# Seven products for four in a part of the first MLP layer of the last two token groups

## The chip, the cores and the metric

The kernel runs on one core of a Trainium2 chip. Times are device microseconds (us) of that core from launch to end; the number compared is the median over several runs. The profile is one further execution with the hardware profiler; its span reaches from the first to the last instruction.

## The reference

Causal attention with 16 extra "beacon" keys, then an MLP with a quick gelu. The operands come as float32.

```python
B, H, S, Nb, D = (8, 8, 576, 16, 64)
scores = scale * np.matmul(q, k_all.transpose(0, 1, 3, 2))   # k_all: beacon_k, k
scores = np.where(causal, -1000000000.0, scores)
a = np.exp(scores - scores.max(-1, keepdims=True))
a /= a.sum(-1, keepdims=True) + 1e-09
attn_out = np.matmul(a, v_all)
...
x = attn_out.transpose(0, 2, 1, 3).reshape(B * S, H * D)     # 4608 x 512
h = x @ w_in                                                 # w_in  512 x 2048
g = h * (1.0 / (1.0 + np.exp(-1.702 * h)))
return g @ w_out                                             # w_out 2048 x 512
```

## The kernel before

The kernel is one stream of instructions for each engine, written out by a planner while the program is built. Each piece of work is an `op` with an engine, an estimated duration, the pieces that it depends on, a priority and at times a due time. `Plan.run` (L65) goes through them as a list scheduler would and so fixes the order on each engine; the semaphores between engines follow from the tiles read and written. On the chip nothing is reordered: an engine takes its instructions in that order and waits where an operand is late.

**Attention** goes in 16 sets (8 batches, two halves of the heads). A set's scores are made in chunks by TensorE (`e_qk`, L448) into one tile of four PSUM banks, `s`; ScalarE takes the exponent into an SBUF tile `E` (L466), of which there are three in rotation; GpSimd masks (L490); VectorE sums over keys (L502); TensorE multiplies with V (`e_av`, L539), and VectorE normalizes into `xT` (L574), which holds x transposed, in f16, for four batches of tokens. There are 55 chunks. VectorE also transposes Q and K (L429).

**The MLP** goes in ten groups of tokens: groups 0 and 1 of 256, groups 2 to 9 of 512. The first layer (`e_m1`, L593, with its matmul at L604) makes 16 tiles of 128 rows of h for a group, each from four matmuls of 512 columns, each tile in one of the four other PSUM banks ("the ring", `u`). ScalarE's gelu (L625) writes the tile into `g`. The second layer of groups 2 to 9 is already done by Strassen's scheme in Winograd's form (`products`, L958): VectorE makes sums of quarters of g in `sA` (L669, f16; one set of tiles, so a group's sums begin when the group before has had its products), sums of quarters of w_out in `tB` once, TensorE makes seven products (`e_prod`, L704, L718), each of 16 matmuls of 256 columns, and they are put together by one scaled copy on ScalarE (L729) and seven joins on VectorE (L734), which add a product in PSUM to a part in SBUF. Four DMAs a group then store the result (L741).

**What sets the order around the change.** `QUOTAS` (L271) holds, for groups 2 to 9, the number of chunks after which the group's first layer is opened; while it is open ("inside"), no further chunk is issued and first-layer tiles go ahead of second-layer ones. `choose` (L191) picks TensorE's next piece: chunks first, then attention values that have waited for 7000 ns, then first-layer tiles if inside, otherwise first- and second-layer pieces in turn. `ring_free` (L55) gives the bank of the ring that is free first. `due_of` (L750) spreads the sets between `T_ATT0` and `T_ATT1` (L746): Q and K transposes are due 12 us before a set, loads of Q and K 22 us, of V 12 us. `NEAR` (L14) is how long VectorE is kept for urgent work, `IDLE` (L15) how long TensorE may stand idle before a group is opened early, `TDUE` (L948) when the sums of w_out are due. Groups 8 and 9 are tokens 3584 to 4095 and 4096 to 4607; both need attention of the last batch.

Of the kernel before, what the change touches and what calls it, by code (L numbers as in the profile page):

```python
# [10 lines left out]
ALU = mybir.AluOpType  # L11


NEAR = 500  # L14
IDLE = 800  # L15


class Op:
# [6 lines left out]
class Plan:  # L25
# [4 lines left out]

    def __init__(self, ring):
        self.ops = []
        self.bank = [None] * ring
        self.tiles = {}
        self.closers = {}
        self.quota = {}
# [15 lines left out]
        self.ops.append(o)  # L52
        return o

    def ring_free(self):  # L55
        best = None
        for i, key in enumerate(self.bank):
            t = 0
            for c in self.closers[key] if key is not None else ():
                t = None if t is None or c.start is None else max(t, c.end + 60)  # L60
            if t is not None and (best is None or t < best[0]):
                best = (t, i)
        return best

    def run(self):  # L65
# [8 lines left out]
        group, inside, ntile, nchunk = min(self.quota), False, 0, 0  # L74
        firsts = {}
        for o in self.ops:
            if o.kind == "m1":
                firsts.setdefault(o.pr, o)

        left_of = {}  # L80
        for o in self.ops:
# [3 lines left out]
        def allowed(o):  # L85
            if o.kind == "m2" and o.ring not in self.tiles:
                if sum(left_of[k] > 0 for k in self.tiles if k in left_of) >= 2:
                    return False
            if o.kind == "m1":
                return o.pr < group or (o.pr == group and (inside or group not in self.quota))  # L90
            if o.kind == "qk":
                return not inside
            if o.table is not None and o.table != table:
                return due_of_table[table] == 0
            return True
# [3 lines left out]
        while todo:  # L99
            best = None  # L100
            if not inside and group in self.quota:
                f = firsts[group]
                inside = nchunk >= self.quota[group] and f.left == 0
            slot = self.ring_free()
            ringt = slot[0] if slot else None
            for e, cand in avail.items():
                t = None
                for o in cand:
                    if not allowed(o):
                        continue  # L110
                    r = max(o.ready, o.due)
                    if o.ring is not None and o.ring not in self.tiles:
                        if ringt is None:
                            continue
                        r = max(r, ringt)
                    if t is None or r < t:
                        t = r
                if t is not None:
                    t = max(t, free[e])
                    if best is None or t < best[0]:  # L120
                        best = (t, e)
            assert best is not None, [(o.name, o.eng) for o in self.ops if o.start is None][:40]
            t, e = best
            if e == "PE" and not inside and t > free[e] + IDLE and group in self.quota:
                f = firsts[group]
                if f.left == 0 and f.ready <= t:
                    inside = True
                    continue
            ok = []
            for o in avail[e]:  # L130
                if not allowed(o):
                    continue
                r = max(o.ready, o.due)
                if o.ring is not None and o.ring not in self.tiles:
                    if ringt is None:
                        continue
                    r = max(r, ringt)
                if r <= t:
                    ok.append(o)
            if e == "PE":  # L140
                o = self.choose(ok, t, mode, last, free, inside)
            else:
                o = min(ok, key=lambda o: (o.pr, o.ready, o.seq))
                if e == "DVE" and o.pr > 0:
                    near = [x for x in avail[e] if x.pr == 0 and max(x.ready, x.due) <= t + NEAR]
                    if near:
                        o = min(near, key=lambda o: (o.ready, o.seq))
                        t = max(t, o.ready, o.due)
            dur = o.dur
            if e == "PE":  # L150
                if o.mode != mode:
                    dur += 95 + 0.75 * tail / 2.4
                mode, last, tail = o.mode, o.kind, o.tail
                if o.ring is not None and o.ring not in self.tiles:
                    self.tiles[o.ring] = slot[1]
                    self.bank[slot[1]] = o.ring
            if o.kind == "m1":
                ntile += 1 if o.pr == group else 0
                if inside and ntile == 16:
                    group, inside, ntile = group + 1, False, 0  # L160
# [12 lines left out]
            o.start, o.end = t, t + dur  # L173
            free[e] = o.end
            avail[e].remove(o)
            order.append(o)
            todo -= 1
            for u in o.users:
                u.left -= 1
                lat = self.LAT[o.eng] if u.eng != o.eng or o.eng == "Q" else 0  # L180
                if u.eng == "Q":
                    lat = 300 if o.eng == "SP" else 1200
                elif o.name == "bk" and o.eng != "DVE":
                    lat = 2500
# [6 lines left out]
    def choose(self, ok, t, mode, last, free, inside):  # L191
# [12 lines left out]
                return av  # L204
        if qk:
            return qk
        late = first(("av",), lambda o: o.ready + 7000 <= t)
        if late:
            return late
        m1, m2 = first(("m1",)), first(("m2",))  # L210
# [8 lines left out]
def kernel(  # L219
# [11 lines left out]
    nc = tc.nc  # L231
# [36 lines left out]
    w2t = cst.tile([P, NNT, DMODEL], F16, tag="w2", name="w2")  # L268
    XR = 4 * S
    NPL, NPE, GEL = 2, 10, 2  # L270
    QUOTAS = (19, 28, 38, 42, 48, 55, 55, 55)  # L271
    HM, HN = 256, NNT // 2
    xT = cst.tile([P, NKT, XR], F16, tag="xT", name="xT")
    sA = [cst.tile([P, HN, HM], F16, tag=f"sA{i}", name=f"sA{i}") for i in range(3)]
    tB = [cst.tile([P, HN, HM], F16, tag=f"tB{i}", name=f"tB{i}") for i in range(3)]
# [80 lines left out]
    rings, Es, ss, gts, zs, zsum = {}, {}, {}, {}, {}, {}  # L356

    plan = Plan(RING)

    def ring_tile(key):  # L360
        if key not in rings:
            i = plan.tiles[key]
            rings[key] = psu.tile([P, 512], F32, tag=f"u{i}", name=f"u{i}")
        return rings[key]


# [223 lines left out]
        GROUPS.append((t, min(NTOK, t + 512)))  # L590
    NG = len(GROUPS)

    def e_m1(g, n0, n1):  # L593
        t0, t1 = GROUPS[g]
        w = t1 - t0
        if g not in gts:
            gts[g] = gp.tile([P, NNT, 512], F16, tag="g", name="g")
        u = ring_tile(("m1", g, n0))
        for nt in range(n0, n1):
            o = (nt - n0) * w  # L600
# [75 lines left out]
    def e_t(i, eng):  # L676
# [9 lines left out]
        else:  # L686
            add(eng, t3, b22, b12, ALU.subtract)

    def quarter(g, i, j):
        return gts[g][:, HN * j : HN * (j + 1), HM * i : HM * (i + 1)]  # L690

# [169 lines left out]
    def values(s):  # L861
# [96 lines left out]
    def products(g):  # L958
        eng = "POOL" if g < SDVE else "DVE"
        sd = {}  # L960
        for n0 in range(0, HN, SQ):
            n1 = n0 + SQ
            prev = []
            for i in range(4):
                deps = prev + done.get(g - 1, [])
                for n in range(n0, n1):
                    deps += [gates[(g, n)], gates[(g, n + HN)]]
# [8 lines left out]
        def prod(p):  # L976
            prev = []
            for n0 in range(0, HN, SQ):
                deps = list(prev)
                if lhs[p] is not None:  # L980
                    deps.append(sd[(lhs[p], n0)])
                else:
                    deps += [gates[(g, n + (HN if p in (2, 4) else 0))] for n in range(n0, n0 + SQ)]
                if rhs[p] is not None:
                    deps.append(tds[rhs[p]])
                o = op(
# [34 lines left out]
        store(c12, "m", 0, 1)  # L1021
        ends[g] = c12

    def mlp(g):
        if g == NPL and NPL < NPE:
            weights()
# [108 lines left out]
```

## Time and profile before

| | us |
|---|---|
| median of 3 runs (331.37 to 331.89) | 331.48 |
| the profiled execution | 331.71 |
| its span | 330.0 |
| PE busy | 311.5 (94%) |
| DVE busy | 237.5 (72%) |
| ACT busy | 203.6 (62%) |
| POOL busy | 116.9 (35%) |
| granted TensorE clock | 1.000 |

PE is TensorE's matmuls, PEld its weight loads, DVE VectorE, ACT ScalarE, POOL GpSimd, SP the engine that issues the stores. The end of a matmul is modelled, and matmuls overlap, so PE's busy time alone doesn't say whether it is at its peak; the distance between starts in a long run of equal matmuls does. A row names the line, the operation, what it writes and reads and in which shape, how often, and in brackets how long the engine stood idle before it and what ended that. The order of the stages from 245 us on, as TensorE's timeline has it:

| stage | from (us) | to (us) |
|---|---|---|
| first layer of group 7, with the key sums of set 15 between | 245.8 | 260.1 |
| three products of group 7's second layer | 260.1 | 266.3 |
| attention values of set 15 | 266.3 | 267.8 |
| first layer of group 8 | 267.8 | 281.6 |
| the other products of group 7 | 281.6 | 287.7 |
| first layer of group 9 | 287.7 | 301.5 |
| second layer of group 8 | 301.5 | 313.8 |
| second layer of group 9 | 313.8 | 326.2 |
| last join, store, end | 326.2 | 330.0 |

### The profile page before, as it was taken

The numbers are of one execution on the slowest core, as the hardware profiler recorded it, in microseconds if no ns is written. First come the engines' busy times: TensorE is split into PE (matmuls) and PEld (weight loads), VectorE is DVE, ScalarE is ACT, GpSimd is POOL, SyncE is SP. The second block draws the span as 40 slices with busy tenths as digits, with TensorE's granted clock in tenths as the row PEclk, the third lists the DMA queues.
The fourth block names the chain that finished last, engine by engine and source line by source line (L and its number), as shares of the span: only waits on it lengthen the run. The fifth ranks groups of instructions, "written<-read, shape, count | busy, mean of one in ns | idle before, by whom it ended". The sixth has DMA issues, their size and how long they took to land. (4 is left out here: it accounts for less than half of the span.)

```text
span 330.0 us, 9837 instructions
## 1 busy us (share of the span) xinstructions
PE 311.5 (94%) x4288; PEld 210.9 (64%) x4288; DVE 237.5 (72%) x478; ACT 203.6 (62%) x234; POOL 116.9 (35%) x178
## 2 busy tenths in 40 slices
PE   0699899999999999999999999999999999999995
PEld 0477666545885467646878877447774664746884
DVE  4847959796998788987999589978896630460484
ACT  1676487787767786777758586858677427175000
POOL 8765557572238205360427046702422000000000
PEclk9999999999999999999999999999999999999999
DMA  7999999569017903392149623930120000110122
GB/s 126 161 205 208 200 178 156 83 105 130 29 41 140 145 2 82 89 129 50 47 95 127 85 53 89 127 85 2 34 96 3 2 32 2 46 51 2 66 96 95
DMA packets 58219, 28.81 MB, mean 87 GB/s; under 512 B 41280, under 2 KB 53568, under 8 KB 58176
## 3 DMA queue, kind: packets, MB, share of 16 engines
q0 software_dynamic: 47552, 18.49, 47.7%
q1 hardware_dynamic: 10560, 9.69, 8.9%
q8 instruction: 33, 0.54, 0.7%
q14 instruction: 10, 0.08, 0.1%
q10 hardware_dynamic: 64, 0.01, 0.0%
HBM read 37.22 MB, written 9.44 MB: 141 GB/s over the span
## 5 line engine op out<-in xcount | busy, mean ns | idle before, releaser
L604 PE MATMUL u<-xT,w 128*128 128x512 f16 (+1 forms) x704 | 130.7, 343 | 2.1 <-DVE g L637 1.1
L469 ACT ACTIVATE E<-s 128x2048 f16<-128x2048 f32 (+4 forms) x66 | 98.8, 1514 | 42.7 <-PE s L458 42.0
L604 PEld LDWEIGHTS <-w 128*128 128x128 f16 x704 | 68.0, 98 | 58.5 <-issue 3.2
L625 ACT ACTIVATE g<-u 128x512 f16<-128x512 f32 x128 | 74.4, 598 | 43.2 <-PE u L604 43.0
L490 POOL TENSOR_SCALAR_AFFINE_SELECT E<-E 128x512 f16<-128x512 f16 (+3 forms) x78 | 52.0, 689 | 119.9 <-ACT E L469 116.2
L734 DVE SCALAR_TENSOR_TENSOR osb<-u,osb 128x512 f32<-128x512 f32 x56 | 37.4, 680 | 40.5 <-PE u L718 26.9
L718 PEld LDWEIGHTS <-g 128*128 128x128 f16 x512 | 48.6, 98 | 7.3 <-issue 0.2
L458 PE MATMUL s<-qT,kT 32*128 32x32 f16 (+20 forms) x1376 | 35.9, 235 | 11.7 <-DVE qT L429 10.3
L718 PE MATMUL u<-w,g 128*128 128x256 f16 x384 | 46.0, 273 | 0.0
L458 PEld LDWEIGHTS <-kT 32*128 32x128 f16 x1376 | 26.0, 95 | 29.1 <-issue 14.7
L718 PEld LDWEIGHTS <-sA 128*128 128x128 f16 x384 | 36.4, 98 | 4.9
L718 PE MATMUL u<-tB,sA 128*128 128x256 f16 x256 | 31.3, 273 | 0.0
L389 POOL DMA_DIRECT2D vb<-in_v_dram x32 | 27.3, 866 | 2.5 <-DMA kn<-in_k_dram 1.5
L545 PE MATMUL u<-E,vb 128*32 128x352 f16 (+8 forms) x928 | 27.7, 267 | 0.0
L580 DVE TENSOR_TENSOR xT<-u,rz 128x352 f16<-128x352 f32 (+2 forms) x52 | 24.9, 518 | 1.7 <-PE u L545 1.1
L508 DVE TENSOR_TENSOR zs<-zs,E 128x1344 f16<-128x1344 f16 (+2 forms) x36 | 23.5, 652 | 3.1 <-POOL E L490 0.5
L545 PEld LDWEIGHTS <-vb 128*32 128x32 f16 (+1 forms) x928 | 20.1, 98 | 5.4 <-issue 1.3
L429 DVE STREAM_TRANSPOSE kT<-kn 128x576 f32<-128x576 f32 x16 | 20.1, 1258 | 4.4 <-PE s L458 2.8
L669 DVE TENSOR_TENSOR sA<-g 128x512 f16<-128x512 f16 x32 | 12.8, 417 | 12.2 <-ACT g L625 11.9
L429 DVE STREAM_TRANSPOSE qT<-qn 128x576 f32<-128x576 f32 x16 | 20.0, 1249 | 2.2 <-PE s L458 1.8
L557 DVE STREAM_TRANSPOSE zt<-u 128x352 f32<-128x352 f32 (+2 forms) x32 | 13.8, 459 | 9.0 <-PE u L545 8.9
L718 PE MATMUL u<-tB,g 128*128 128x256 f16 x128 | 16.3, 273 | 0.0
(44 smaller groups left out, 229.1 us busy)
## 6 DMA issues: line engine op xcount, KB each, us to landing
out_dram<-osb SPq DMA_DIRECT2D x36, 256.0 KB, 2.2
kn<-in_k_dram POOLq DMA_DIRECT2D x16, 288.0 KB, 5.6
qn<-in_q_dram POOLq DMA_DIRECT2D x16, 288.0 KB, 6.3
vb<-in_v_dram POOLq DMA_DIRECT2D x24, 128.0 KB, 5.2
w<-in_moe_w_in_dram POOLq DMA_DIRECT2D x8, 256.0 KB, 9.2
w<-in_moe_w_out_dram POOLq DMA_DIRECT2D x4, 512.0 KB, 14.0
vb<-in_v_dram POOLq DMA_DIRECT2D x8, 112.0 KB, 3.7
vb<-in_v_dram POOLq DMA_DIRECT2D x8, 80.0 KB, 5.0
```

Source lines behind the costliest of these rows:

```text
L389: nc.gpsimd.dma_start(out=t[0 : hi - lo, j, h0:h1, :], in_=v[b, h0:h1, lo:hi, :].rearrange("h n d -> n h d"),)
L429: nc.vector.transpose(out=f32(dst.rearrange("p n e -> p (n e)")).rearrange("p (r t) -> p t r", t=TR), in_=f32(src[:, :]).rearrange("p (t c ...
L458: nc.tensor.matmul(sc[:, h, o : o + w], kT[s % NB2][r : r + 32, j * P : (j + 1) * P, d], qT[s % NB2][r : r + 32, a : a + w, d], start=(d = ...
L469: nc.scalar.activation(out=Es[s][:, :, c0:c1], in_=ss[i][:, :, o : o + c1 - c0], func=AFT.Exp, scale=0.125,)
L490: nc.gpsimd.affine_select(out=blk, in_=blk, compare_op=ALU.is_ge, fill=0.0, base=off + (Nb if j == 0 else 0), pattern=[[0, Q], [1, w]], ch ...
L508: nc.vector.tensor_tensor(out=t, in0=E[:, :, Z0:S] if i == 1 else t, in1=E[:, :, wcol[i] : wcol[i] + S - a], op=ALU.add,)
L545: nc.tensor.matmul(u[32 * h : 32 * h + 32, a:e], lhs, src[0:kw, h, col : col + e - a], start=first, stop=last,)
L580: nc.vector.tensor_tensor(out=xT[:, 2 * hs + x : 2 * hs + x + n, t0 : t0 + w], in0=rings[("av", s, x, half)][:, 0 : n * w].rearrange("p (n ...
L604: nc.tensor.matmul(u[:, o + a - t0 : o + e - t0], w1t[:, kp, nt * P : (nt + 1) * P], xT[:, kp, a % XR : (e - 1) % XR + 1], start=(kp == 0) ...
L625: nc.scalar.activation(out=gts[g][:, n0:n1, 0:w], in_=rings[("m1", g, n0)][:, 0 : n * w].rearrange("p (n w) -> p n w", n=n), func=AFT.Gelu ...
L718: nc.tensor.matmul(u[:, HM * mt : HM * (mt + 1)], lhs[:, n, mt * P : (mt + 1) * P], rhs[:, n, :], start=(n == 0 and mt == 0), stop=(n == H ...
L734: nc.vector.scalar_tensor_tensor(out=osbs[(g, dst)][:, :], in0=rings[("p", g, p)][:, :], scalar=scale_of(g), in1=osbs[(g, src)][:, :], op0 ...
```

## The change

In groups 8 and 9 a part of the first layer is made by the same scheme of seven products. h transposed, for one group, is a matrix of 2048 x 512; it is cut into the halves of the 2048 rows (index i), the halves of the 512 tokens (index j) and, along the 512 that are summed over, into two halves. `FIRST` names slices: slice d takes rows 256 d to 256 d + 255 of each half, so four of a group's 16 tiles. Group 8 has slices 0 and 2 done this way, group 9 slices 0, 1 and 2; the other slices stay with `e_m1`. A product (`e_first`) is four matmuls of 256 columns into one bank. The banks are the four of the score tile `s`, taken over once the last exponent has been read out of them (`plan.gate`, `late_s`). Four sums of quarters of w_in (`e_wsum`, once) and four of x (`e_xsum`, once a group) are made in f16 by VectorE, and the parts of a slice (m, a, u) are kept in f32; all of them lie in the three `E` tiles, after the attention values of sets 13, 14 and 15 have been read. Per slice there is one copy on ScalarE, seven joins on VectorE, and four gelus, which read the part in SBUF.

The planner changes too: two lists of free banks; from group 8 on (`MIX`) first-layer tiles of any group are allowed and taken in turn with second-layer pieces (`LATE1` = 0); and its constants are other ones.

```diff
-NEAR = 500
-IDLE = 800
+NEAR = 560
+IDLE = 3000
+MIX = 8
+LATE1 = 0
...
             if o.kind == "m1":
+                if group >= MIX:
+                    return True
                 return o.pr < group or (o.pr == group and (inside or group not in self.quota))
...
-                o = self.choose(ok, t, mode, last, free, inside)
+                o = self.choose(ok, t, mode, last, free, inside and (group < MIX or LATE1))
...
-        late = first(("av",), lambda o: o.ready + 7000 <= t)
+        late = first(("av",), lambda o: o.ready + 5000 <= t)
...
-    QUOTAS = (19, 28, 38, 42, 48, 55, 55, 55)
+    QUOTAS = (20, 27, 33, 33, 47, 54, 55, 55)
+    FIRST = {8: (0, 2, ), 9: (0, 1, 2, )}
...
+            if i < RING:
+                rings[key] = psu.tile([P, 512], F32, tag=f"u{i}", name=f"u{i}")
+            else:
+                if not late_s:
+                    late_s.append(pss.tile([P, Q, 512], F32, tag="s", name="s"))
+                rings[key] = late_s[0][:, i - RING, :]
...
+    def late_tile(i):
+        if i not in lateE:
+            lateE[i] = ep.tile([P, Q, ETOT], F16, tag="E", name="E")
+        return lateE[i][:, :, :].rearrange("p q e -> p (q e)")
...
+        for t in range(2):
+            n = (2 * d + t) * P
+            for k in range(2):
+                nc.tensor.matmul(
+                    u[:, HM * t : HM * (t + 1)],
+                    lhs[:, k, n : n + P],
+                    rhs[:, k, :],
+                    start=(t == 0 and k == 0),
+                    stop=(t == 1 and k == 1),
+                )
+    def e_fcopy(g, d):
+        nc.scalar.copy(out=part(d, "m"), in_=rings[("n", g, d, 1)][:, :])
+    def e_fjoin(g, d, p, src, dst):
+        nc.vector.tensor_tensor(
+            out=part(d, dst), in0=rings[("n", g, d, p)][:, :], in1=part(d, src), op=ALU.add
+        )
...
-    T_ATT0, T_ATT1 = 17000, 249000
+    T_ATT0, T_ATT1 = -1000, 245000
...
-                op("DVE", 75 + 0.517 * 4 * w, deps + sums[-1:], lambda i=i: e_zadd(s, i), pr=3, name="zadd")
+                op("DVE", 75 + 0.6 * 4 * w, deps + sums[-1:], lambda i=i: e_zadd(s, i), pr=3, name="zadd")
...
-    SQ, SDVE, TDUE = 2, 0, 60000
+    SQ, SDVE, TDUE = 2, 0, 70000
...
+        prod(1)
+        m = op(
+            "ACT", 480, [last[1], used.get("m")] + free, lambda: e_fcopy(g, d), pr=1,
+            closes=("n", g, d, 1), name="fcopy",
+        )
+        prod(2)
+        c11 = join(2, "m", "a", [m, used.get("a")] + free)
+        ga = gelu("a", 0, 0, c11)
+        prod(6)
+        u2 = join(6, "m", "m", [c11])
+        prod(7)
+        u3 = join(7, "m", "u", [u2, used.get("u")])
+        prod(4)
+        c21 = join(4, "u", "a", [u3, ga])
+        ga = gelu("a", 1, 0, c21)
+        prod(5)
+        u4 = join(5, "m", "m", [u3], False)
+        c22 = join(5, "u", "u", [c21, u4])
+        gu = gelu("u", 1, 1, c22)
+        prod(3)
+        c12 = join(3, "m", "m", [u4])
+        gm = gelu("m", 0, 1, c12)
...
+            if n0 % HN // SQ in FIRST.get(g, ()):
+                if n0 < HN and n0 % SQ == 0:
+                    first_quarters(g, n0 // SQ, xs, old)
+                continue
...
+    plan.gate = exps[(len(CHUNKS) - 1, len(CHUNKS[-1]) - 1)]
```

More of the change, by code (lines that the diff above doesn't have):

```diff
@@ L32, in __init__ @@
         self.ops = []
-        self.bank = [None] * ring
+        self.bank = [None] * (ring + 4)
+        self.ring = ring
+        self.gate = None
         self.tiles = {}
@@ L53, in op, with ring_free @@
         return o
-    def ring_free(self):
+    def ring_free(self, late):
         best = None
-        for i, key in enumerate(self.bank):
-            t = 0
+        if late and self.gate.start is None:
+            return None
+        for i in range(self.ring, self.ring + 4) if late else range(self.ring):
+            key = self.bank[i]
+            t = self.gate.end + 200 if late else 0
             for c in self.closers[key] if key is not None else ():
@@ L73, in run @@
         table, due_of_table = "e", {"e": 0, "g": 0}
-        group, inside, ntile, nchunk = min(self.quota), False, 0, 0
-        firsts = {}
+        group, inside, nchunk = min(self.quota), False, 0
+        firsts, count = {}, {}
         for o in self.ops:
@@ L78, in run @@
                 firsts.setdefault(o.pr, o)
+                count[o.pr] = count.get(o.pr, 0) + 1
         left_of = {}
@@ L103, in run @@
                 inside = nchunk >= self.quota[group] and f.left == 0
-            slot = self.ring_free()
-            ringt = slot[0] if slot else None
+            slots = [self.ring_free(late) for late in (False, True)]
             for e, cand in avail.items():
@@ L112, in run @@
                     if o.ring is not None and o.ring not in self.tiles:
-                        if ringt is None:
+                        slot = slots[o.ring[0] == "n"]
+                        if slot is None:
                             continue
-                        r = max(r, ringt)
+                        r = max(r, slot[0])
                     if t is None or r < t:
@@ L134, in run @@
                 if o.ring is not None and o.ring not in self.tiles:
-                    if ringt is None:
+                    slot = slots[o.ring[0] == "n"]
+                    if slot is None:
                         continue
-                    r = max(r, ringt)
+                    r = max(r, slot[0])
                 if r <= t:
@@ L154, in run @@
                 if o.ring is not None and o.ring not in self.tiles:
+                    slot = slots[o.ring[0] == "n"]
                     self.tiles[o.ring] = slot[1]
@@ L157, in run @@
             if o.kind == "m1":
-                ntile += 1 if o.pr == group else 0
-                if inside and ntile == 16:
-                    group, inside, ntile = group + 1, False, 0
+                count[o.pr] -= 1
+                if inside and count[group] == 0:
+                    group, inside = group + 1, False
             if o.kind == "m2":
@@ L358 @@
     plan = Plan(RING)
+    late_s = []
     def ring_tile(key):
@@ L362, in ring_tile @@
             i = plan.tiles[key]
-            rings[key] = psu.tile([P, 512], F32, tag=f"u{i}", name=f"u{i}")
+            if i < RING:
[4 more added lines that the diff above has]
+                rings[key] = late_s[0][:, i - RING, :]
         return rings[key]
@@ L591, with group_tile @@
     NG = len(GROUPS)
+    def group_tile(g):
+        if g not in gts:
+            gts[g] = gp.tile([P, NNT, 512], F16, tag="g", name="g")
+        return gts[g]
     def e_m1(g, n0, n1):
@@ L595, in e_m1 @@
         w = t1 - t0
-        if g not in gts:
-            gts[g] = gp.tile([P, NNT, 512], F16, tag="g", name="g")
+        group_tile(g)
         u = ring_tile(("m1", g, n0))
@@ L687, in e_t, with wsum, xsum @@
             add(eng, t3, b22, b12, ALU.subtract)
+    lateE = {}
+    def late_tile(i):
+        if i not in lateE:
+            lateE[i] = ep.tile([P, Q, ETOT], F16, tag="E", name="E")
+        return lateE[i][:, :, :].rearrange("p q e -> p (q e)")
+    def wsum(i):
+        t = late_tile(0)[:, 2048 * i : 2048 * (i + 1)] if i < 3 else late_tile(1)[:, 0:2048]
+        return t.rearrange("p (k n) -> p k n", k=2)
+    def xsum(g, i):
+        o = 2048 * (1 + g % 2) + 512 * i
+        return late_tile(1)[:, o : o + 512].rearrange("p (k w) -> p k w", k=2)
@@ new lines, in part, with wq, xq, e_wsum @@
+    def part(d, x):
+        i = 3 * (d % 2) + "mau".index(x)
+        return f32(late_tile(2)[:, 1024 * i : 1024 * (i + 1)])
+    def wq(i, j):
+        return w1t[:, 2 * j : 2 * j + 2, DFF // 2 * i : DFF // 2 * (i + 1)]
+    def xq(g, i, j):
+        t0 = (GROUPS[g][0] + HM * j) % XR
+        return xT[:, 2 * i : 2 * i + 2, t0 : t0 + HM]
+    def e_wsum(i):
+        s1, s2, s4, s3 = (wsum(x) for x in range(4))
+        if i == 0:
+            add("DVE", s1, wq(1, 0), wq(1, 1), ALU.add)
+        elif i == 1:
+            add("DVE", s2, s1, wq(0, 0), ALU.subtract)
+        elif i == 2:
+            add("DVE", s4, wq(0, 1), s2, ALU.subtract)
+        else:
+            add("DVE", s3, wq(0, 0), wq(1, 0), ALU.subtract)
@@ new lines, in e_xsum, with e_first @@
+    def e_xsum(g, i):
+        t1, t2, t4, t3 = (xsum(g, x) for x in range(4))
+        if i == 0:
+            add("DVE", t1, xq(g, 0, 1), xq(g, 0, 0), ALU.subtract)
+        elif i == 1:
+            add("DVE", t2, xq(g, 1, 1), t1, ALU.subtract)
+        elif i == 2:
+            add("DVE", t4, xq(g, 1, 0), t2, ALU.subtract)
+        else:
+            add("DVE", t3, xq(g, 1, 1), xq(g, 0, 1), ALU.subtract)
+    def e_first(g, d, p):
+        u = ring_tile(("n", g, d, p))
+        lhs, rhs = {
+            1: (wq(0, 0), xq(g, 0, 0)),
+            2: (wq(0, 1), xq(g, 1, 0)),
+            3: (wsum(2), xq(g, 1, 1)),
+            4: (wq(1, 1), xsum(g, 2)),
+            5: (wsum(0), xsum(g, 0)),
+            6: (wsum(1), xsum(g, 1)),
+            7: (wsum(3), xsum(g, 3)),
+        }[p]
+        for t in range(2):
[8 more added lines that the diff above has]
+                )
@@ new lines, in e_fcopy, with e_fgelu @@
+    def e_fcopy(g, d):
[4 more added lines that the diff above has]
+        )
+    def e_fgelu(g, d, x, i, j):
+        n0 = 2 * d + HN * i
+        nc.scalar.activation(
+            out=group_tile(g)[:, n0 : n0 + 2, HM * j : HM * (j + 1)],
+            in_=part(d, x).rearrange("p (t w) -> p t w", t=2),
+            func=AFT.Gelu_apprx_sigmoid,
+        )
@@ L966, in products @@
                 for n in range(n0, n1):
-                    deps += [gates[(g, n)], gates[(g, n + HN)]]
+                    deps += gate(g, n) + gate(g, n + HN)
                 d = 336
@@ L982, in prod @@
                 else:
-                    deps += [gates[(g, n + (HN if p in (2, 4) else 0))] for n in range(n0, n0 + SQ)]
+                    for n in range(n0, n0 + SQ):
+                        deps += gate(g, n + (HN if p in (2, 4) else 0), 1 if p == 4 else 0)
                 if rhs[p] is not None:
@@ L1022, in products, with first_quarters, prod, join @@
         ends[g] = c12
+    wsums = []
+    def first_quarters(g, d, xs, old):
+        every = [(x, h) for x in range(3) for h in range(2)]
+        if not wsums:
+            deps = [avs.get((NSET - 3, x, h)) for x, h in every]
+            for i in range(4):
+                more = [avs.get((NSET - 2, x, h)) for x, h in every] if i == 3 else []
+                wsums.append(op("DVE", 1130, deps + more + wsums[-1:], lambda i=i: e_wsum(i), pr=3, name="wsum"))
+        if (g, 0) not in xsums:
+            deps = xs + [avs.get((NSET - 2, x, h)) for x, h in every]
+            deps += [o for o in m1s.get(g - 2, []) if o.ring[0] == "n"]
+            for i in range(4):
+                xsums[(g, i)] = o = op("DVE", 336, deps, lambda i=i: e_xsum(g, i), pr=2, name="xsum")
+                deps = [o]
+        free = [avs.get((NSET - 1, x, h)) for x, h in every]
+        lhs = {1: None, 2: None, 3: 2, 4: None, 5: 0, 6: 1, 7: 3}
+        rhs = {1: None, 2: None, 3: None, 4: 2, 5: 0, 6: 1, 7: 3}
+        last, used = {}, fused.get(d % 2, {})
+        def prod(p):
+            deps = xs + old + [w for n in (2 * d, 2 * d + 1, 2 * d + HN) for w in w1_of[n]]
+            deps += [wsums[lhs[p]]] if lhs[p] is not None else []
+            deps += [xsums[(g, rhs[p])]] if rhs[p] is not None else []
+            last[p] = op(
+                "PE", 4 * 109, deps, lambda: e_first(g, d, p), kind="m1", pr=g,
+                ring=("n", g, d, p), mode="m", name=f"m1.{g}.{d}.{p}",
+            )
+            m1s.setdefault(g, []).append(last[p])
+        def join(p, src, dst, deps, closes=True):
+            return op(
+                "DVE", 605, [last[p]] + deps, lambda: e_fjoin(g, d, p, src, dst), pr=2,
+                closes=("n", g, d, p) if closes else None, name="fjoin",
+            )
+        def gelu(x, i, j, dep):
+            o = op("ACT", 520, [dep] + old, lambda: e_fgelu(g, d, x, i, j), pr=1, name="fgelu", table="g")
+            for n in (2 * d + HN * i, 2 * d + HN * i + 1):
+                gates.setdefault((g, n), {})[j] = o
+            return o
+        prod(1)
+        m = op(
+            "ACT", 480, [last[1], used.get("m")] + free, lambda: e_fcopy(g, d), pr=1,
+            closes=("n", g, d, 1), name="fcopy",
+        )
+        prod(2)
[15 more added lines that the diff above has]
+        gm = gelu("m", 0, 1, c12)
+        fused[d % 2] = {"m": gm, "a": ga, "u": gu}
@@ L1024, in mlp, with gate @@
+    fused, xsums = {}, {}
+    def gate(g, n, i=None):
+        got = gates[(g, n)]
+        if isinstance(got, dict):
+            return list(got.values()) if i is None else [got[i]]
+        return [got]
     def mlp(g):
```

## The prediction

> **What bounds the kernel now.** I read the windows first, with borders at the ends of the stages that the TensorE timeline shows, and from the last attention product (267.8 us) on. Columns: stretch, its length, then busy us and instructions of PE, PEld, DVE, ACT, POOL, and the clock.
>
> ```profile
> 267.80:281.70 13.90, 13.90 (x73) 6.36 (x66) 0.60 (x2) 8.96 (x15) 0.00 (x0) 1.00 0.00 1
> 281.70:287.80 6.10, 6.10 (x58) 5.46 (x57) 2.67 (x4) 0.60 (x1) 0.00 (x0) 1.00 0.12 43
> 287.80:301.60 13.80, 13.80 (x66) 6.26 (x65) 6.06 (x17) 8.96 (x15) 0.00 (x0) 1.00 0.12 40
> 301.60:313.80 12.20, 12.20 (x114) 10.93 (x113) 4.05 (x6) 1.20 (x2) 0.00 (x0) 1.00 0.13 44
> 313.80:326.20 12.40, 12.37 (x114) 10.84 (x111) 9.93 (x23) 0.60 (x1) 0.00 (x0) 1.00 0.25 85
> 326.20:330.00 3.80, 0.00 (x0) 0.00 (x0) 0.69 (x1) 0.00 (x0) 0.00 (x0) 1.00 0.39 138
> ```
>
> The rows are: first layer of group 8; the rest of group 7's second layer; first layer of group 9; second layers of 8 and of 9; the closing join and store. PE has no gap, while DVE is busy 24.0 of 62.2 us. The chain of waits says the same: from 287.9 on it is matmuls alone, then one join.
>
> ```profile
> 287.90 13.81 PE u L604 x64
> 301.72 24.47 PE u L718 x224
> 326.18 0.02 issue
> 326.21 0.69 DVE osb L734
> ```
>
> It also gives rates: 13.81/64 = 215.8 ns for a 512-column first-layer matmul and 24.47/224 = 109.2 ns for a 256-column Strassen one (a matmul's own row of 379 or 273 ns includes its drain). In this stage a matmul less is time less, as long as every operand is there.
>
> Before it PE is nearly as full. Its waits up to 240 us are one short table; of the matmul's waits only these are over 1 us:
>
> ```profile
> PE s L458 <- DVE qT L429: 10.3, 2, 8.2
> PE s L458 <- ACT E L469: 1.4, 3, 0.6
> PE u L604 <- DVE g L637: 1.1, 1, 1.1
> PE u L604 <- ACT g L625: 1.0, 3, 0.4
> ```
>
> The first is the start (operands arrive), the rest could be reordered away.
>
> **What the Trainium skill says.** "TensorE: Matmul & The Clock Gate", section "Wait — 56ns, not 53.3ns?", gives N/2.4 GHz plus about 2.5 ns: 215.8 and 109.2 ns, exactly the two rates above. "VectorE: DVE Perf Modes", section "The perf-mode tier table", says that a two-tensor operation with a PSUM operand runs at one element a cycle, and with 16-bit SBUF operands at two; the trace has 0.69 us for a 512-column join and 0.42 for a 512-column f16 sum. "PSUM — Partial Sum Buffer", section "PSUM bank collisions raise a hardware error", says two engines may not be in one bank at once, so a product's bank is shut until its last reader is through; no run here shows a collision. "ScalarE: Activation LUTs", section "Table sets: the hidden batching unit", says copy is in every set; the trace agrees: the scaled copy at 303.50 between gelus has no table load beside it.
>
> **The change, part by part.**
>
> *Matmuls.* FIRST takes two of four column pairs of group 8 and three of group 9. One pair is 4 tiles x 4 matmuls of 512 columns, 16 x 215.8 = 3.453 us; as seven products of four 256-column matmuls it is 28 x 109.2 = 3.058. Five pairs save 5 x 0.395 = 1.98 us of PE. Each 256-column matmul has its own weight load (98 ns), which stays beneath 109 as in the second layer.
>
> *Added on DVE.* Seven joins a pair, 35 in all. The nearest row is L734, same shape and types from PSUM and SBUF:
>
> ```profile
> 324.46 1.29 DVE L734 SCALAR_TENSOR_TENSOR osb<-u,osb 128x512 f32<-128x512 f32 x2 [1.05 <-PE u L718]
> 314.59 1.42 DVE L669 TENSOR_TENSOR sA<-g 128x512 f16<-128x512 f16 x4
> ```
>
> Two back to back take 1.29 with the drain, so 0.60 apart (1.29 - 0.69); one that must wait occupies 0.69. 35 joins are 21.2 us at 0.605, 24 at 0.69. Four sums in f16 take (1.42 - 0.42)/3 = 0.333 apart. Input sums: 8 x 0.333 = 2.7. Weight sums: 4 of 128x2048, for which L669 has 1.21 to 1.30 us: 5.0. Together 29 to 32 us. The weight sums have the lowest priority and need only set 13's memory (the fourth also set 14's); from 246 to 267.8 DVE is busy 14.3 of 21.8, so 7.5 free us cover them. If not, products 5, 6, 7 and 3 wait for them while 1, 2 and 4 don't need a weight sum.
>
> *Added on ACT.* Five copies at L729's 0.60 = 3.0 us; gelus keep their number (20 of 32 now read SBUF: 52 cycles at 1.2 GHz or 43 ns more each by the table in "The TRN2 errata" of the VectorE page, an estimate; from nothing to 0.9 us in all). ACT is busy 20.3 of 58.4 us there: free.
>
> *Waits that come with it.* A product waits for its bank (last join done), its sums and the norms of its tokens; behind it on PE stands all other work, in order. A join waits for its product; behind it on DVE stand sA sums and second-layer joins, and PE's later products wait for those. A gelu waits for a join; behind it stand gelus that hold the ordinary ring's banks. So what matters is DVE's room. From T0 = 267.8 PE has: rest of P7 6.1, plain first-layer tiles 12 x 0.863 = 10.4, Strassen tiles 5 x 3.06 = 15.3, P8 12.2, P9 12.2: 56.2 us. Up to P9 that is 44.0 us. DVE in these 44 us: norms 1.5, input sums 2.7, new joins 21.2, joins of P7 (5) and P8 (7) 7.3, sA sums of group 8 5.3 (16 x 0.333): 38.0 us, 86% full, 6.0 us spare. P9 is as before: its sA sums begin once P8 is done, beneath its products 1 and 2. Mixing (m1 and m2 in turn from group 8 on) supplies the filler: 28 second-layer pieces a group between products. A product and a piece are 0.87 us of PE; one join, and a quarter of a second-layer join, 0.76 of DVE. It fits, tightly. I take 0.5 us of PE gaps (bounds: 0, since spare exists, and a saving beyond the matmuls has no source there; 4.3, in rival A).
>
> *Banks and memory.* The score tile's four banks are free after the last exp (246.3), 20 us before T0, so the gate costs nothing. The sums and parts lie in E buffers that av of sets 13 to 15 has left; only the first copy waits for av 15, which ends at T0 and which group 8 needs anyway.
>
> *Retimed order.* New QUOTAS, due times (attention 4 us earlier at its end, 18 at its start), NEAR, IDLE, TDUE, 5000 for 7000, and zadd's price change the order everywhere, adding no work. Values a little earlier move T0 forward, which gives the Strassen part more filler (P7). Loads due earlier put 0.56 to 0.9 us issues ahead of masks on POOL; POOL is 35% busy. The waits after the start sum to about 3.6 us (PE's idle from 20 to 220 us in windows: 1.34 + 0.74 + 0.81 + 0.75). The order can win at most that; it can lose as much by a wrong order of early loads. I take a gain of 0.4.
>
> *Plan code.* All else runs when the program is built: nothing.
>
> **Sum.** Span 330.0 - 1.98 + 0.5 - 0.4 = 328.1. The end after PE's last matmul (3.8 us: join, store, landing) is unchanged. The profiled execution took 331.71, 1.71 over its span; the shown median is 331.48, 0.23 below it. So 328.1 + 1.71 - 0.23 = 329.6 us.
>
> **Rivals.**
>
> *A. DVE becomes the bound of the stretch (slower).* The same place, T0 to P9. DVE has 6.0 us to spare; 35 new joins eat it when each costs 6.0/35 = 0.17 us more than 0.605, that is from a step of 0.78 us on. A join that always waits for PE takes 0.69 plus a hand-over; at 0.90 the stretch is over by 35 x 0.295 - 6.0 = 4.3 us, at 0.86 by 2.9. With 1.98 saved that is 331.5 - 2.0 + 2.9 = 332.4 to 333.8; I name 333.0. For it: before, joins come alone with about 1 us idle before them. Against: that idle is PE's pace of 1.75 us a product, not DVE's; back to back they run at 0.60.
>
> *B. The new order costs what the matmuls save.* PE's 3.6 us of idle before the tail grow by 2: 331.5, no change. For it: the due times move by up to 18 us early, where DMA engines are fullest. Against: the first 20 us carry loads that are due at once in both kernels.
>
> *C. The order gains besides.* Half of the 3.6 us goes and no gap comes: 330.0 - 1.98 - 1.8 + 1.48 = 327.7. For it: all the table's later waits are at group openings, which quotas place. Against: each is only 0.3 to 1.1 us.
>
> *D. Not what it says:* if the banks' readers were tracked as one tile, the four products would run one by one, about 1.3 us each instead of 0.44. The old score tile is always freed whole, so before doesn't show it; partial tracking within other tiles (g read by pieces while written) speaks against it. It would act as A, and is counted there.
>
> **Chances.** Forecast 0.52, A with D 0.24, B 0.12, C 0.12. About 0.2% (0.66 us) is what can be told from no change: under 330.8 faster, over 332.1 slower. Forecast gives 0.50 faster and 0.02 same; A 0.01, 0.03 and 0.20; B 0.01, 0.08 and 0.03; C 0.12 faster: 0.64, 0.13, 0.23. The range goes from halfway into C to the middle of A, 327.9 to 333.0; the likeliest case's own is 328.7 to 330.7.
>
> **What would show it.** Right: the matmuls of the new line x140 and L604's 512-column ones 80 fewer; PE rows after the last av without waits; DVE about 85% busy from there to P9; new joins at about 0.6 us steps; the last matmul at about 324 us of the span. A shows as PE waiting on the new joins or on sA, with DVE at 95% or more; B as longer PE waits before 245 us; C as their absence. I am wrong if the tail holds PE waits of 2 us or more, or if the work before it shifts by more than 1 us.

## The result, and the profile after

The changed kernel takes 349.55 us (median of 4 runs, 349.48 to 349.93) against 331.69 us before (median of 4; the 331.48 above is of 3 of them): 1.0542 times as long, with a 95% interval of 1.0524 to 1.056. It is slower by 17.9 us where the prediction had it 2 us faster. The profiled execution took 349.93 us, its span is 348.2.

These are the same stages in the windows of the changed kernel. Columns: stretch, its length, then busy us and instructions of PE, PEld, DVE, ACT, POOL, and the clock; the last two numbers are the DMA engines' share and GB/s. Group 7's second layer is finished before 277.1 here; the second row reaches from the first product of the new kind to the last one, the third to the last matmul.

```profile
250.00:277.10 27.10, 26.68 (x333) 18.49 (x331) 19.29 (x43) 10.92 (x15) 2.91 (x3) 1.00 0.08 28
277.10:328.60 51.50, 38.34 (x293) 27.66 (x286) 35.28 (x66) 20.11 (x33) 0.00 (x0) 1.00 0.08 27
328.60:344.40 15.80, 15.80 (x130) 12.39 (x127) 11.72 (x26) 3.80 (x7) 0.00 (x0) 1.00 0.15 51
344.40:348.20 3.80, 0.01 (x1) 0.00 (x0) 0.69 (x1) 0.00 (x0) 0.00 (x0) 0.79 0.40 138
```

PE, which had no gap here before, is busy 38.3 of 51.5 us, and DVE is not full either: 35.3. So neither engine is the bound; they wait for each other. Below is TensorE's timeline of a few us in that stretch, then VectorE's of the same few (start, length, then engine, line, operation, operands; in brackets the idle time before and who ended it):

```profile
302.12 0.60 PE L774 MATMUL s<-E 128*128 128x256 f16 x4 [0.41 <-DVE E L786]
302.55 0.60 PE L827 MATMUL u<-w,g 128*128 128x256 f16 x4
302.99 0.60 PE L774 MATMUL s<-E,w 128*128 128x256 f16 x4
303.42 0.60 PE L827 MATMUL u<-tB,sA 128*128 128x256 f16 x4
304.37 0.60 PE L774 MATMUL s<-E 128*128 128x256 f16 x4 [0.35 <-DVE E L786]
304.80 0.60 PE L827 MATMUL u<-tB,sA 128*128 128x256 f16 x4
305.75 0.60 PE L774 MATMUL s<-xT,E 128*128 128x256 f16 x4 [0.34 <-DVE E L786]
```

```profile
303.63 0.69 DVE L786 TENSOR_TENSOR E<-s,E 128x512 f32<-128x512 f32 x1 [0.63 <-PE s L774]
304.23 0.41 DVE L692 TENSOR_TENSOR sA<-g,sA 128x512 f16<-128x512 f16 x1
305.00 0.69 DVE L786 TENSOR_TENSOR E<-s,E 128x512 f32<-128x512 f32 x1 [0.36 <-PE s L774]
```

L774 is a product, L786 a join. The join at 303.63 begins 0.04 us after the product that started at 302.99 has ended, and the product at 304.37 begins 0.05 us after that join. A product, then a join, then a product: 304.37 to 305.75 is 1.38 us = 0.60 + 0.03 + 0.69 + 0.05 (rounded), in which PE can put only one second-layer piece (0.44). Without the wait, a product and a piece take 0.87. About 0.5 us is lost a product, and there are 35 of them. With four banks a product should have three others to go on with. These are three of the matmuls' waits over the whole span (us in total, times, longest); only the wait for the first operands, 11.2 us at the start, is larger:

```profile
PE s L774 <- DVE E L786: 10.1, 18, 1.2
PE s L477 <- ACT E L488: 3.8, 6, 2.0
PE s L774 <- ACT E L783: 3.0, 4, 1.0
```

The first and the third make 13.1 us, which is PE's idle time in the stretch (51.5 - 38.3 = 13.2). The second is outside the tail: the wait for the exponent before the next scores was 1.4 us before and is 3.8. This is part of the end of the chain of waits, which was matmuls alone before:

```profile
325.51 0.70 DVE E L786
326.26 0.61 PE s L774 x4
326.95 0.70 DVE E L786
327.69 0.60 PE s L774 x4
```

The built program agrees. The table has instructions of one slice (the second of group 9), each with the last product or join that its semaphores name, in the changed kernel and in the experiment e1 below:

```
             changed kernel     e1
product 7    join 2             a join of the slice before
join 6       product 4          product 6
product 5    join 7             join 2
join 4       product 5          product 4
product 3    join 4             join 6
```

Join 6 should need product 6 alone; it waits for product 4, which is in another bank and was merely issued before it. The same program is finer in SBUF: joins 6 and 7 write parts m and u of an `E` tile while a gelu that stands ahead of them in the program reads part a of that tile, and they carry no wait for ScalarE.

### The profile page after: what moved, and what is told of

It is laid out like the page before. It is cut to its first block, busy times and chain, and to the rows that moved or that the text cites. A ratio compares the mean times of both kernels' runs of the same rounds, so it can differ in the third digit from the quotient of the medians.

```text
span 348.2 us, 10016 instructions
## 1 busy us (share of the span) xinstructions
PE 312.7 (90%) x4348; PEld 216.2 (62%) x4348; DVE 266.4 (77%) x525; ACT 209.2 (60%) x241; POOL 115.2 (33%) x178
## 4 chain that ended last, share of the span: by engine, by line
PE 70%; DVE 13%; ACT 8%; DMA 3%; issue 3%; SPq 1%; POOL 1%; DVEq 0%; ACTq 0%
PE u L627 26%; PE u L827 21%; PE s L477 8%; PE u L564 7%; DVE E L786 6%; PE s L774 5%; ACT E L488 5%; DMA bkf<-in_beacon_k_dram 3%; PE u L672 3%; ACT L648 1%; DVE osb L843 1%; DVE qT L448 1%; SPq L427 1%; DVE zs L527 1%; DVE rz L587 1%
## 5 line engine op out<-in xcount | busy, mean ns | idle before, releaser
L627 PE MATMUL u<-xT,w 128*128 128x512 f16 (+1 forms) x624 | 115.0, 336 | 2.3 <-ACT g L648 1.1
L509 POOL TENSOR_SCALAR_AFFINE_SELECT E<-E 128x512 f16<-128x512 f16 (+3 forms) x78 | 50.6, 670 | 138.3 <-ACT E L488 136.3
L627 PEld LDWEIGHTS <-w 128*128 128x128 f16 x624 | 60.0, 98 | 46.2 <-issue 3.6
L648 ACT ACTIVATE g<-u 128x512 f16<-128x512 f32 x108 | 63.1, 598 | 31.2 <-PE u L627 30.7
L477 PE MATMUL s<-qT,kT 32*128 32x32 f16 (+20 forms) x1376 | 35.7, 234 | 15.0 <-DVE qT L448 11.2
L827 PE MATMUL u<-w,g 128*128 128x256 f16 x384 | 48.5, 273 | 0.0
L786 DVE TENSOR_TENSOR E<-s,E 128x512 f32<-128x512 f32 x35 | 23.6, 689 | 16.0 <-PE s L774 15.5
L827 PE MATMUL u<-tB,sA 128*128 128x256 f16 x256 | 32.8, 273 | 0.0
L527 DVE TENSOR_TENSOR zs<-zs,E 128x1344 f16<-128x1344 f16 (+2 forms) x36 | 24.3, 676 | 2.7 <-POOL E L509 0.5
L792 ACT ACTIVATE g<-E 128x512 f16<-128x512 f32 x20 | 12.4, 627 | 21.6 <-DVE E L786 21.6
L527 DVE TENSOR_TENSOR zs<-E 128x1856 f16<-128x1856 f16 x12 | 15.6, 1300 | 6.8 <-ACT E L488 5.3
```

The costliest lines, as they stand in the source:

```text
L477: nc.tensor.matmul(sc[:, h, o : o + w], kT[s % NB2][r : r + 32, j * P : (j + 1) * P, d], qT[s % NB2][r : r + 32, a : a + w, d], start=(d = ...
L509: nc.gpsimd.affine_select(out=blk, in_=blk, compare_op=ALU.is_ge, fill=0.0, base=off + (Nb if j == 0 else 0), pattern=[[0, Q], [1, w]], ch ...
L527: nc.vector.tensor_tensor(out=t, in0=E[:, :, Z0:S] if i == 1 else t, in1=E[:, :, wcol[i] : wcol[i] + S - a], op=ALU.add,)
L627: nc.tensor.matmul(u[:, o + a - t0 : o + e - t0], w1t[:, kp, nt * P : (nt + 1) * P], xT[:, kp, a % XR : (e - 1) % XR + 1], start=(kp == 0) ...
L648: nc.scalar.activation(out=gts[g][:, n0:n1, 0:w], in_=rings[("m1", g, n0)][:, 0 : n * w].rearrange("p (n w) -> p n w", n=n), func=AFT.Gelu ...
L786: nc.vector.tensor_tensor(out=part(d, dst), in0=rings[("n", g, d, p)][:, :], in1=part(d, src), op=ALU.add)
```

## The experiments

All were compared with the kernel before on the same chip (medians of 331.67 to 331.78 us there). **Theory T** has two parts. The four banks are slices of one tile, and a PSUM tile is guarded as a whole: each join waits for the last product issued and each product for the last join issued. That costs the tail some 17 us. The new order of the rest costs some 3 us more. **Rival A** is the prediction's: VectorE is too full for 35 joins, whatever the banks.

**e1, four tiles.** Order, products and joins as in the changed kernel; the score pool is closed after its last reader and four tiles of one bank take its place.

```diff
-    pss = ctx.enter_context(tc.tile_pool(name="pss", bufs=1, space=bass.MemoryType.PSUM))
...
+    scores = ctx.enter_context(ExitStack())
+    pss = scores.enter_context(tc.tile_pool(name="pss", bufs=1, space=bass.MemoryType.PSUM))
...
-                if not late_s:
-                    late_s.append(pss.tile([P, Q, 512], F32, tag="s", name="s"))
-                rings[key] = late_s[0][:, i - RING, :]
+                if not late_s:
+                    scores.close()
+                    late_s.append(ctx.enter_context(
+                        tc.tile_pool(name="psl", bufs=1, space=bass.MemoryType.PSUM, reuse_waits="tile")
+                    ))
+                rings[key] = late_s[0].tile([P, 512], F32, tag=f"l{i}", name=f"l{i}")
```

> The changed kernel with one edit: the four late banks are four tiles of a pool of their own instead of slices of one score tile. Order, products, joins and memory are the same. Theory T (the banks are one tile, so each product waits for the join before it and each join for the product before it): the 17 us of PE gaps between the last attention product and the last matmul go, leaving at most 1 us; 349.6 - 17 + 1 = 333 us, and the new joins no longer start at the end of the next product. Rival A (VectorE is too full for 35 joins whatever the banks): the gaps stay, 345 us or more.

Measured: 333.69 us, ratio 1.0058 (1.0038 to 1.0078), where the ratio is to the kernel before and the brackets hold its 95% interval, as in all that follow. The same stretch of work in its windows, with the columns as above:

```profile
277.70:312.70 35.00, 34.73 (x294) 27.70 (x285) 33.08 (x66) 19.16 (x32) 0.00 (x0) 1.00 0.09 32
312.70:328.50 15.80, 15.80 (x130) 12.45 (x128) 11.91 (x27) 4.43 (x8) 0.00 (x0) 1.00 0.20 67
```

35.0 us against 51.5, with the same products, joins and order: 16.5 us is the price of the one tile. Of this 13 us were PE's idle time; the rest is in its busy time, 38.3 against 34.7, where a group of four matmuls that stands alone shows 0.60 us and in an unbroken run takes 0.44. PE is now busy 34.7 of 35.0, and DVE does its 33 us of work in 35. Joins run back to back (three in 1.88 us, so 0.60 apart):

```profile
300.05 1.28 DVE L790 TENSOR_TENSOR E<-l,E 128x512 f32<-128x512 f32 x2
301.24 0.68 DVE L847 SCALAR_TENSOR_TENSOR osb<-u,osb 128x512 f32<-128x512 f32 x1
301.84 1.88 DVE L790 TENSOR_TENSOR E<-l,E 128x512 f32<-128x512 f32 x3
```

Rival A falls for five slices. The 2 us that e1 is still above the kernel before don't come from PE's waits in the tail.

**e2, the new order alone.** All first layers are plain (FIRST empty, no mixing of first and second layers); of the change only the constants are left.

```diff
-MIX = 8
+MIX = 99
-    FIRST = {8: (0, 2, ), 9: (0, 1, 2, )}
+    FIRST = {}
```

> The changed kernel without any slice done in seven products and without mixing (FIRST empty, MIX beyond the last group): all first layers are plain, so only the new constants are left. Theory T says that the order costs about 3 us before the tail (the last attention values end at 277.2 with group 7's second layer done, against 267.8 + 6.1 = 273.9): 331.5 + 3.3 = 334.8 us. The rival, that the order is neutral and all is lost at the products, says 331.5.

Measured: 335.83 us, ratio 1.0127 (1.0102 to 1.0151). The order costs 4.1 us by itself. The matmuls' waits show a part; the wait below was 1.4 us before:

```profile
PE s L477 <- ACT E L488: 5.8, 7, 2.0
```

With this order ScalarE also changes its table between exponent and gelu 14 times instead of 12 (1.28 us each), as it does in the changed kernel. From e2 to e1 the five slices bring 335.83 - 333.69 = 2.1 us. The clock is in both medians. In e1 as in e2, two of four executions had a mean granted clock of 0.993 to 0.995 (e1 334.1 and 334.3 us, e2 336.3 and 336.8). The other two had 0.997 or more (e1 333.0 and 333.3, e2 334.8 and 335.4), as the changed kernel had in all four. From these alone the order costs 3.4 us and the slices bring 2.0; the last section comes back to this clock.

**e3 and e4, the old order.** The scheme with the constants of the kernel before (mixing stays), once with four tiles (e3) and once with one (e4). This order needs two repairs: a sum of w_in names only the tile that it writes, and the first transposition of a set's sums waits for the reciprocal two halves back:

```diff
-        s1, s2, s4, s3 = (wsum(x) for x in range(4))
         if i == 0:
-            add("DVE", s1, wq(1, 0), wq(1, 1), ALU.add)
+            add("DVE", wsum(0), wq(1, 0), wq(1, 1), ALU.add)
...
-                    "DVE", 65 + 1.045 * cols, [avs[(s, x, half)]], lambda h=half: e_z1(s, h), pr=0, closes=key, name="z1"
+                    "DVE", 65 + 1.045 * cols, [avs[(s, x, half)], z2s.get(two_back(s, half))], lambda h=half: e_z1(s, h), pr=0, closes=key, name="z1"
```

> The scheme with five slices and four separate tiles, but with the constants of the kernel before (500, 800, old QUOTAS, due times, 7000, 0.517), and two small repairs of dependencies that this order needs: the sum of weights names only the tile that it writes, and the first transposition of a set's sums waits for the reciprocal two halves back. Theory T: 331.5 - 2.0 + 0.5 = 330.0 us, faster than before. Rival A: 342 us or more.

> As e3, but the four late banks are slices of one tile as in the changed kernel. Theory T: the tail loses its 17 us again, less the 3.3 us that the order cost: 346 us. If the loss came from the new order starving the tail: 331 to 333 us.

Measured: e3 331.26 us, ratio 0.9983 (0.9976 to 0.9989); e4 346.8 us, ratio 1.0459 (1.0443 to 1.0475). The one tile costs 15.5 us in this order too, so the new order is not what starves the tail. The old order takes 2.4 us off e1. e3 stays 1.3 us short of its expectation. The last scores start at 243.6 us in e3 and in the kernel before, so the shortfall lies behind them. From 240 to 260 us e3's PE is idle for 0.68 us where the kernel before has no gap: the planner opens group 7 at once after the last scores, and the ring fills before ScalarE is through with the exponent and its table. Up to the last matmul its PE is busy 81.44 us against 82.57, which is 1.1 us less where the matmul count says 2.0; why it isn't more stays open.

**e8, one slice in one tile.** As e4, with FIRST = {9: (0,)}.

> e4 (old order, banks in one tile) with a single slice, 0 of group 9, instead of five. If the loss comes slice by slice (17 us for five, 3.4 us each): 331.5 - 0.4 + 3.4 = 334.5 us. If filler between the products hides a single slice: 331.5.

Measured: 335.49 us, ratio 1.0113 (1.0098 to 1.0129). One slice of seven products costs 3.8 us, though there is filler on both sides of it; five cost 15. Of the 3.8 us, 0.68 is the idle time from 240 to 260 us that e3 has too. So the loss goes with the number of products, about 3 us a slice.

**e7, the one tile without the scheme.** The kernel before, its ordinary ring as slices of one tile:

```diff
-            rings[key] = psu.tile([P, 512], F32, tag=f"u{i}", name=f"u{i}")
+            if not whole:
+                whole.append(psu.tile([P, RING, 512], F32, tag="u", name="u"))
+            rings[key] = whole[0][:, i, :]
```

> The kernel before with one edit: the four banks of the ordinary ring are slices of one tile kept for the whole program, instead of four tiles. No work is added or taken away. If a tile is tracked as a whole, each first-layer tile waits for the gelu of the one before it: 0.86 us become about 0.86 + 0.60 + 0.3, for some 130 tiles, so 331.5 + 115 = 445 us, give or take 40. If banks within a tile are told apart: 331.5.

Measured: 572.15 us (one execution). The timeline of PE, its weight loads and ScalarE:

```profile
471.74 1.02 PE L608 MATMUL u<-xT,w 128*128 128x512 f16 x4 [0.69 <-ACT g L629]
471.74 0.74 PEld L608 LDWEIGHTS <-w 128*128 128x128 f16 x4 [0.96 <-issue]
472.80 0.60 ACT L629 ACTIVATE g<-u 128x512 f16<-128x512 f32 x1 [1.11 <-PE u L608]
473.45 1.02 PE L608 MATMUL u<-xT,w 128*128 128x512 f16 x4 [0.69 <-ACT g L629]
```

Tile and gelu alternate at 1.71 us where plain tiles took 0.86. That step was expected at 1.76. The total is 127 us over the expectation. That counted first-layer tiles alone, but second-layer products and attention values use the ring as well: second-layer matmuls wait for joins another 26 us, for instance. The mean granted clock of this execution is also only 0.937; the shares were not added up. No work was added, so the mechanism stands without the scheme of seven products.

**e5, eight slices.** e3 with FIRST = {8: (0, 1, 2, 3), 9: (0, 1, 2, 3)}, where rival A should hold.

> e3 (old order, four tiles) with all four slices of both groups in seven products instead of five of eight. It saves 3 x 0.395 = 1.2 us more of PE and adds 21 joins. By the sum of the prediction VectorE then has 38.0 + 21 x 0.605 = 50.7 us of work in 42.8 us of PE work before group 9's second layer: if that sum is right, VectorE becomes the bound there and the time is 331.3 - 1.2 + 8 = 338 us. If VectorE has more room than the sum says: 330 us.

Measured: 340.01 us, ratio 1.0251 (1.0237 to 1.0265). The stretch from the first product to the last:

```profile
274.70:323.00 48.30, 44.81 (x379) 35.48 (x372) 47.63 (x94) 23.04 (x39) 0.00 (x0) 1.00 0.09 30
```

VectorE is busy 47.6 of 48.3 us, and matmuls wait for joins and sums. Rival A is right about eight slices. The expectation was 338 us, 2.0 too low.

**e6 and e9, a better order, with and without slices.** Six slices in four tiles, and constants chosen for them; e9 has the same constants and no slice. Against e3:

```diff
-    QUOTAS = (19, 28, 38, 42, 48, 55, 55, 55)
+    QUOTAS = (19, 37, 41, 44, 54, 55, 55, 55)
-    FIRST = {8: (0, 2), 9: (0, 1, 2)}
+    FIRST = {8: (0, 1, 2), 9: (0, 1, 2)}
...
-    T_ATT0, T_ATT1 = 17000, 249000
+    T_ATT0, T_ATT1 = 22000, 243000
...
-    SQ, SDVE, TDUE = 2, 0, 60000
+    SQ, SDVE, TDUE = 2, 0, 65000
```

> Four tiles with six slices (0, 1, 2 of both groups) and an order of its own: QUOTAS (19, 37, 41, 44, 54, 55, 55, 55), T_ATT0 and T_ATT1 22000 and 243000, TDUE 65000, the rest as before. One slice more than e3 saves 0.4 us and fewer openings late in attention may save up to 1 us of waits: 330.0 us; if the order makes new waits, 332.

> e6 with FIRST empty: the same order constants, all first layers plain. If the seven products give what the matmul count says, six slices are worth 6 x 0.395 = 2.4 us: 329.4 + 2.4 = 331.8 us, no change against before, and the gain of e6 is the scheme's. If e6's gain came from its order: 329.5.

Measured: e6 329.44 us, ratio 0.993 (0.9918 to 0.9943), faster than both kernels; e9 331.52 us, ratio 0.9994 (0.9985 to 1.0002). So the gain is the scheme's: 331.52 - 329.44 = 2.1 us for six slices, 0.35 each against 0.395 by the matmul count. The two ran on different chips; against the kernel before on its own chip e6 is 2.2 us lower and e9 0.3, which makes 2.0. In e6's windows, from the first product to the last of its tail:

```profile
266.60:312.80 46.20, 46.20 (x400) 38.29 (x393) 44.93 (x89) 21.83 (x38) 0.00 (x0) 1.00 0.12 41
312.80:323.90 11.10, 11.10 (x102) 9.69 (x99) 6.83 (x15) 1.08 (x2) 0.00 (x0) 1.00 0.14 49
```

PE has no gap while VectorE is busy 97% of the stretch: six slices are close to the most that fits.

**e10, one constant.** The kernel before with IDLE 3000 for 800.

> The kernel before with IDLE 3000 for 800 and nothing else: TensorE may stand idle for up to 3 us for the next scores before a group is opened early. e2 lost 4.1 us with all new constants, and 4.4 us more of its waits are on the exponent before the next scores than before. If this constant is what does it: 334 to 335 us. If the cost comes from the others: 331.7.

Measured: 339.45 us, ratio 1.0234 (1.022 to 1.0248): 7.7 us for one constant, more than the 4.1 of all together and far above the 335 expected. In its profile PE is idle for 6.3 us more than before (24.8 against 18.5), while ScalarE changes its table 12 times as before; the last section shows a further part of the loss. So the constants can't be added up one by one; the others take back part of it, and which ones was not tried.

## Why the prediction was wrong

**The step that failed** is the wait in the part on what comes with the change: "A product waits for its bank (last join done)". It waits for the last join issued, in whatever bank, because the four banks are one tile; and a join waits in the same way for the last product issued. The sum took 0.5 us of PE gaps for this stretch; e1 against the changed kernel puts the term at 16.5 us. Rival D named the mechanism, and priced a product at 1.3 us, close to the measured 1.38. It failed in what was done with that number. It was folded into A, whose 333.0 us it doesn't have: at 1.38 - 0.87 = 0.51 us over a product and a piece, 35 products give 17.9 us, within 1.4 of the 16.5. And the reason against it, that pieces of g are read while others are written, is about an SBUF tile; it says nothing of a PSUM tile, and in this very program the two are treated differently.

**The second wrong term** is the retimed order: a gain of 0.4 us was taken, with a gain and a loss of 3.6 us as bounds. e2 has a loss of 4.1 us, just outside these bounds (3.4 without the two executions at the lower clock, just inside). They came from the waits that the order of before had, and a new order can make new ones; two more table changes were not thought of at all. Rival B had the sign, with 2 us. This term alone would have made the forecast gain a loss; it is about a fifth of what happened.

**What held.** The matmul count: 2.0 us for five slices; e2 against e1 gives 2.1, though in the old order (e3) only 0.4 us are left over the kernel before. The step of the joins: 0.60 back to back. The sum of VectorE's work: it said that five slices fit, tightly, at 86%; they do, with VectorE busy 33.1 of 35.0 us in e1, where group 7's second layer is no longer there as filler. Carried on to eight slices the sum gave 338 us, and e5 took 340.0. The covers held too: the weight sums and the extra ScalarE work made no wait worth naming in e1, whose products wait 0.3 us in all, and the end after the last matmul is 3.8 us as before. The gelus that read SBUF take 0.627 us against 0.598 from PSUM, 29 ns more where the estimate had 43. One reading was wrong and changes nothing: the scaled copy at 303.50 is not between gelus, since the last gelu starts at 301.75; the copy at 262.00 is (gelus at 260.25 and 268.94), and no table load stands there either.

**The sum as measured:** 331.7 + 4.1 (order) - 2.1 (slices, e2 to e1) + 15.9 (one tile, e1 to the changed kernel) = 349.6. The three terms are steps from one run to the next, so they must add up; what speaks for them is that the windows give 16.5 us and e3 to e4 15.5 for the last one, and the matmul count 2.0 for the second. Without the executions at the lower clock they are 3.4, 2.0 and 16.4.

## What to carry to other kernels

Banks that are to be filled and read independently should be tiles of their own; the slices of both PSUM tiles tried here (e4, e7) ran in turn, whatever the planner believed of its banks. A plan's saving counts only once the waits of the built program agree with the plan's idea of what depends on what, and a few lines of its semaphores show that. New constants of a scheduler are to be measured apart from the change that they come with: here they cost twice what the scheme could bring.

## What was not expected of the hardware

In e10 the matmuls after a pause of PE were slower. The next scores start at 105.22 after 1.98 us of idle, the sums at 106.87 after another 1.00:

```profile
105.22 0.65 PE L458 MATMUL s<-qT,kT 32*128 32x400 f16 x24 [1.98 <-ACT E L469]
106.87 0.57 PE L545 MATMUL u<-zs,ones 128*32 128x352 f16 x8 [1.00 <-DVE zs L508]
```

Eight such matmuls took 0.38 us at 97.63, and 0.57 here. The granted clock from 100 to 110 us is 0.83 on average, and 1.00 in the windows around it. Cut finer, it is halved for 3.4 us, after 3.4 us in which PE was busy for a third of the time:

```profile
102.74:106.16 3.42, 1.15 (x40) 0.75 (x33) 3.18 (x5) 2.10 (x2) 0.99 (x3) 1.00 1.01 153
106.16:109.60 3.44, 2.73 (x22) 1.16 (x22) 2.68 (x9) 3.15 (x3) 1.71 (x3) 0.50 0.39 132
```

The Trainium skill describes a clock that falls after an idle window ("TensorE: Matmul & The Clock Gate", section "What's actually happening", about 3.4 us). The length agrees; but the window here was not free of work. Nor does its share of work decide alone. e1 and the changed kernel both make a pause of 2.00 us at one and the same point of the program (some 68 us into the span), with nearly the same work ahead of it; the first two lines below are e1's, the last two the changed kernel's:

```profile
65.06:68.48 3.42, 1.26 (x38) 0.88 (x41) 0.34 (x1) 2.73 (x3) 3.42 (x6) 1.00 1.71 126
68.48:71.90 3.42, 3.42 (x28) 1.40 (x21) 3.33 (x4) 3.01 (x3) 3.28 (x5) 0.50 1.39 194
65.10:68.52 3.42, 1.27 (x27) 0.69 (x26) 0.00 (x0) 3.12 (x3) 3.42 (x6) 1.00 1.81 117
68.52:71.94 3.42, 3.42 (x38) 1.73 (x38) 3.27 (x4) 2.69 (x3) 3.42 (x6) 1.00 1.40 195
```

In e1 the clock was halved, in the changed kernel it stayed at 1.00. What decides was not tried. The executions of e1 and e2 at the lower mean clock may come from this pause, which e2 has too; that is not shown, as e2's profiled execution kept its clock.
